# Expert tiles of the first phase in pairs: first products over 256 tokens at a time

## The chip, the cores and the metric

The kernel runs on one core of one Trainium2 chip. The metric is the device time of one launch in microseconds (us). Five engines work side by side, each through its own list of instructions in a fixed order: PE (TensorE, matrix products; the profile lists its weight loads apart as PEld), DVE (VectorE), ACT (ScalarE), POOL (GpSimd, which here also issues the gathers and scatters) and SP (SyncE, which issues most other DMAs). An instruction that has to wait holds up everything behind it on its engine.

## The reference

There are two stages. The first is a filter in the frequency domain on x of 8 batches x 2496 rows x 256 columns; the second is a mixture of 8 experts, each token going to one of them.

```python
X = rfft(x, axis=1)                              # per batch, along the 2496 rows
Yr = Xr @ w_r - Xi @ w_i + b_r ;  Yi = Xr @ w_i + Xi @ w_r + b_i
Y = shrink(Yr, 0.01) + 1j * shrink(Yi, 0.01)     # sign(v) * max(|v| - 0.01, 0)
y = irfft(Y, n=2496, axis=1)                     # 8 * 2496 = 19968 tokens of 256

e = argmax(y @ w_gate)                           # one expert of 8 for each token
for each expert e, on its own tokens y:
    h = relu(y @ w1[e])                          # 256 -> 1024: the first product
    out = gate * sigmoid(y @ w_output_gate[:, e]) * (h @ w2[e])   # 1024 -> 256: the second
```

## The kernel before

**Stages.** The transform is done as small matrix products, batch by batch, for some 580 us. Its last batch overlaps with the start of the expert stage, which then fills the rest. Filtered tokens y are stored to DRAM (`yd`); logits, the choice of expert and each token's rank in its expert are worked out per batch.

**Tiles of tokens.** The expert stage works on 163 tiles of 128 tokens (T_ALL). Each tile has tokens of one expert only; 163 is enough for any split of the 19968 tokens, and all 163 are always computed. They come in two phases. The first phase (`T_A` = 71 tiles) uses tokens of the first four batches alone, only full tiles of each expert, so that it can start while the last batches are still being transformed. The second phase (`T_B` = 92 tiles) has all other tokens. Within a phase the tiles go by expert. For each phase `routing` makes the lists of token numbers: `plan` (which expert each tile has, at which tile an expert begins), `blocks`, then for 22 columns of each batch one-hot matrices on DVE (L1129, L1130, L1149) that PE multiplies (L1157), then `indices` and `factors` on DVE. The second phase's lists are made while PE works on the first phase's tiles.

**One tile.** POOL gathers its 128 rows of y into `yg` (L1230). DVE finds a power of two per token and ACT and DVE split the row into two f16 parts, `yhl` (L1243 to L1249). SP transposes them with a DMA into `eT` (L1253). First product (`up`, L1295): two halves, each 4 chunks of 128 hidden columns by 6 matmuls. Here the weight chunk (128x128) is the stationary operand and the 128 tokens are the moving one; three f16 products stand for one precise one. Each half fills one PSUM bank of 128x512, which ACT (L1305, relu to f16) and DVE (L1306, the rest in f16) move into `hh`. Second product (L1272): 24 matmuls of 128x256, with the tokens' `hh` stationary. ACT scales the result into `o` (L1281) and POOL scatters it to `out` (L1284).

**Weights.** An expert's weights are 2 MB in f16 parts; three buffers `wbuf0` to `wbuf2` of 2 MB each hold them. Tile t uses one buffer in turn (`wplace`), so when the expert changes, each of the three must be loaded anew; the load's instruction (L1216, one for each half of 1 MB) is issued for every tile and does nothing at run time where the buffer already holds the expert (`cond=g`, the flag in `fl`). The half for the first product waits until the `up` of the tile before it in the same buffer is done, the other half until that tile's second product is done. During the first 8 tiles (`TW`) only buffers 0 and 1 are used; the third lies in memory that the transform frees.

**What sets the order.** A planner (class `Issue`) plays the work through with estimated durations while the program is built: each step asks for an engine with a due time, places in buffers are handed out by `Slots` and `Places`, and the order in which steps are served is the order in which the instructions stand on each engine. So the constants (durations, due times such as `R1`, paces such as `G1`, numbers of places) set an order at build time and nothing at run time.

With the inputs used here the first four batches have 1122, 1344, 1215, 1226, 1333, 1194, 1064 and 1486 tokens for experts 0 to 7.

Of the kernel before, what the change touches and what calls it, by code (L numbers as in the profile page):

```python
# [12 lines left out]
F16 = mybir.dt.float16  # L13
# [21 lines left out]
T_A = -((-(NA * S - E * 127)) // 128)  # L35
T_B = (N - E) // 128 + E - T_A
T_ALL = T_A + T_B

# [91 lines left out]
R1, G1 = 19.93, 1.19  # L130
# [9 lines left out]
EARLY = dict(yg=3, yhl=2, eT=2, hh=1, o=1)  # L140
PLACES = dict(yg=7, yhl=5, eT=6, hh=3, o=7)
TW = 8
# [132 lines left out]
def tile_fft_moe(ctx, tc, x, w_r, w_i, b_r, b_i, w_gate, w_og, w1, w2, f1, f4, cmat, gmat, m16, out, dbg=None):  # L275
# [147 lines left out]
    slots = {k: Slots(n) for k, n in dict(x=XR - 6, s1=S1, A=AN, xt=3, z=2, zhl=ZR, bt=1, bd=1, yt=YR, ol0=OL[0], wr=WR - 1, wsp=SR, ol1=OL[1], fac=10, dg=1).items()}  # L423
    slots.update({k: Places(range(EARLY[k])) for k in EARLY})
    give = lambda k: io.give(slots[k])
# [560 lines left out]
    def shift7(src, add, name):  # L986
        i = small(E, "s7i", I32)
        V.tensor_scalar(i, src, float(add), None, ALU.add)
        V.tensor_scalar(i, i, 7, None, ALU.arith_shift_right)
        f = small(E, name, pool=pc)  # L990
        V.tensor_copy(f, i)
        return f

    def plan(ph):

        if ph == 0:
            fl = shift7(cnt[NA - 1], 0, "fl")
            yield
            pf_ = yield from prefix(fl, "pfA")
            lim = small(E + 1, "lim", pool=pc)  # L1000
            V.tensor_scalar(lim, pf_, float(T_A), None, ALU.min)
# [4 lines left out]
        else:  # L1006
            ce = shift7(cnt[B - 1], 127, "ce")
# [16 lines left out]
        if ph == 0:  # L1024
            route["fl"] = pc.tile([1, T_ALL], I32, name="flg")
            route["ei"] = pc.tile([1, T_ALL], I32, name="ebi")
            V.memset(route["fl"][:, 0:TW + 1], 1)
        V.tensor_copy(route["ei"][:, t0:t0 + n], ev[0:1])
        if ph == 0:
            V.tensor_tensor(route["fl"][:, 2:TW], eb[0:1, 2:TW], eb[0:1, 0:TW - 2], ALU.not_equal)  # L1030
        a = max(t0, TW + 1)
        V.tensor_tensor(route["fl"][:, a:t0 + n], eb[0:1, a:t0 + n], eb[0:1, a - 3:t0 + n - 3], ALU.not_equal)
# [161 lines left out]
    def wplace(t):  # L1194
        return t % 2 if t < TW else (t - TW + 2) % 3

    def before(t):

        return None if t < 2 or t == TW else t - 2 if t < TW else t - 3

    def fetch(r):

        yield "w open"
        for t in range(T_ALL):
            yield "plan", 0 if t < T_A else 1
            if t == TW:
                yield "opened"
            for m in range(2):
                if before(t) is not None:
                    yield ("up", "down")[m], before(t)  # L1210
                def f():
# [4 lines left out]
                    nc.sync.dma_start(W[wplace(t)][:, part], wd[ds(f, 1), :, part].rearrange("a p f -> (a p) f"), cond=g, cond_hint=False)  # L1216

                new = before(t) is None
# [3 lines left out]
    def gathers(r):  # L1222
        yield "w open"
        for t in range(T_ALL):
# [6 lines left out]
            io.go(tile_(t, i, yg, r + 5.6 * t), io.now + 2.6)  # L1231

    def tile_(t, iy, yg, r):
# [3 lines left out]
        fac = small(1, "fac", bufs=10)  # L1237
# [13 lines left out]
        ie = yield slots["eT"]  # L1251
        eT = place("eT", ie, [128, 2, 2, 128], F16)
        yield from move(r - 10, 1.4e5, 1.2, lambda: nc.sync.dma_start(eT.rearrange("p v c n -> p (v c) n"), yhl.rearrange("p v d -> p (v d)"), transpose=True))  # L1253
        yield TAIL
        io.put(slots["yhl"], il)
        yield "w", t, 0
        ih = yield slots["hh"]
        hh = place("hh", ih, [128, 2, 8, 128], F16)
        w = W[wplace(t)][:, :4096].rearrange("p (c h v f) -> p c h v f", c=2, h=2, v=2)
        st["nh", t], st["nu", t] = 0, 0  # L1260
        for half in range(2):
            io.go(up(t, half, w, eT, ie, hh, r))
        yield "hh", t
        yield "w", t, 1
        w = W[wplace(t)][:, 4096:].rearrange("p (i v c d) -> p i v c d", i=4, v=2, c=2)

        def f(i):
            pt = bank(i)
            n = 0
            for fc in range(8):  # L1270
                for v, vw in ((0, 0), (0, 1), (1, 0)):
                    T.matmul(pt[:, :256], hh[:, v, fc], w[:, fc // 2, vw, fc % 2], start=(n == 0), stop=(n == 23))  # L1272
                    n += 1
            return pt

        i, pt = yield "P", r + 4, 2.61, f, True
        io.put(slots["hh"], ih)
        io.set("down", t)
        io_ = yield slots["o"]
        o = place("o", io_, [128, 256], F32)  # L1280
        yield "A", r, 0.47, lambda: A.activation(o, pt[:, :256], AF.Copy, scale=fac)  # L1281
        io.free(i)
        give("fac")
        yield "G", r, 1.0, lambda: G.indirect_dma_start(out=out, out_offset=bass.IndirectOffsetOnAxis(ap=sidx[:, t:t + 1], axis=0), in_=o, in_offset=None, bounds_check=N - 1, oob_is_err=False)  # L1284
        yield 3.6
        io.put(slots["o"], io_)

    def up(t, half, w, eT, ie, hh, r):
        def f(i):
            pt = bank(i)  # L1290
            for j in range(4):
                n = 0
                for dh in range(2):
                    for vw, v in ((0, 0), (0, 1), (1, 0)):
                        T.matmul(pt[:, 128 * j:128 * j + 128], w[:, dh, half, vw, 128 * j:128 * j + 128], eT[:, v, dh], start=(n == 0), stop=(n == 5))  # L1295
# [3 lines left out]
        i, pt = yield "P", r, 1.34, f, True  # L1299
        st["nu", t] += 1  # L1300
        if st["nu", t] == 2:
            io.put(slots["eT"], ie)
# [54 lines left out]
```

## Time and profile before

| | |
|---|---|
| time, median of 3 runs | 1557.16 us (1556.42 to 1560.42) |
| the profiled execution's own time | 1555.91 us |
| its span, first to last instruction | 1554.1 us |
| PE busy | 1440.7 us, 93% of the span |
| DVE, ACT, POOL busy | 63%, 46%, 38% |
| first matmul of the expert stage, last one | 583.2 us, 1546.7 us |
| second product of tile 63 begins | 983.8 us |

The profile was taken from one execution. Times in its rows count from the span's start. A timeline row gives start, length, engine, line of the kernel, operation, out<-in, sizes, how many instructions were merged (x24), and in brackets the idle time of that engine before it with what ended it. "issue" there means that the engine waited for nothing that the profile shows. A group row gives busy time and mean duration of one instruction, then the group's idle time by cause. Names of buffers stand without numbers (`wbuf`, `hh`, `ps` for a PSUM bank).

### The profile page before, as it was taken

Reading aid. Unit: us, or ns where it says so; the run is one execution under the profiler, and the core shown is the slowest. Engines: PE = TensorE matmul, PEld = TensorE weight load, DVE = VectorE, ACT = ScalarE, POOL = GpSimd, SP = SyncE. Lnnn points to the kernel's source line nnn. Section 1 sums busy time; section 2 is a strip of 40 time slices with the busy share of each in tenths; the row PEclk is TensorE's granted clock in tenths of the full one; section 3 lists DMA queues with packets and bytes.
Section 4 is the critical chain, followed back from the end, with each engine's and each line's share of the span. In section 5 each row is a group of like instructions: output and inputs, shape, how many; then the busy total and the mean of one; then the engine's idle time right before and its main releaser. Section 6 shows DMA issues by size and latency. Waiting matters only on the chain. (4 is left out here: it accounts for less than half of the span.)

```text
span 1554.1 us, 45643 instructions
## 1 busy us (share of the span) xinstructions
PE 1440.7 (93%) x17728; PEld 1307.6 (84%) x17728; DVE 973.0 (63%) x2910; ACT 717.0 (46%) x1385; POOL 588.0 (38%) x664
## 2 busy tenths in 40 slices
PE   4899999999899989899999999899999999999998
PEld 4789888787788768788998889788898899889897
DVE  3776777679898876566666657554454554545442
ACT  4666765758566554333333333233333333333332
POOL 0453634446263634133333232334324333333221
PEclk8899999999999999999999999999999999999999
DMA  8879999999999977958746856685673864846820
GB/s 222 200 157 222 225 224 213 208 216 218 213 202 214 201 213 166 255 122 226 228 120 181 216 152 167 202 242 158 156 215 83 230 174 132 230 122 183 216 59 19
DMA packets 330257, 287.64 MB, mean 185 GB/s; under 512 B 277734, under 2 KB 286568, under 8 KB 317753
## 3 DMA queue, kind: packets, MB, share of 16 engines
q1 hardware_dynamic: 313415, 241.50, 63.7%
q0 software_dynamic: 15648, 42.17, 10.6%
q8 instruction: 139, 2.28, 0.6%
q10 hardware_dynamic: 978, 1.06, 0.3%
q14 instruction: 77, 0.63, 0.1%
HBM read 404.52 MB, written 58.91 MB: 298 GB/s over the span
## 5 line engine op out<-in xcount | busy, mean ns | idle before, releaser
L1295 PE MATMUL ps<-eT,wbuf 128*128 128x128 f16 x7824 | 471.5, 220 | 38.3 <-issue 25.1
L1295 PEld LDWEIGHTS <-wbuf 128*128 128x128 f16 x7824 | 451.1, 98 | 52.8 <-issue 34.7
L1272 PE MATMUL ps<-wbuf,hh 128*128 128x256 f16 x3912 | 447.5, 273 | 9.9 <-issue 3.8
L1272 PEld LDWEIGHTS <-hh 128*128 128x128 f16 x3912 | 379.8, 98 | 57.7 <-issue 8.1
L1306 DVE SCALAR_TENSOR_TENSOR hh<-ps,hh 128x512 f16<-128x512 f32 x326 | 222.7, 689 | 290.2 <-ACT hh L1305 259.6
L1284 POOL DMA_INDIRECT out<-o,sidx x163 | 165.3, 1014 | 581.5 <-ACT o L1281 239.4
L1305 ACT ACTIVATE hh<-ps 128x512 f16<-128x512 f32 x326 | 191.4, 596 | 298.2 <-PE ps L1295 213.0
L668 PE MATMUL ps<-whl,xt 128*128 128x256 f16 x1920 | 229.4, 276 | 5.3 <-DVE xt L650 2.2
L668 PEld LDWEIGHTS <-xt 128*128 128x128 f16 x1920 | 190.0, 99 | 42.8 <-DVE xt L650 2.9
L1281 ACT ACTIVATE o<-ps,fac 128x256 f32<-128x256 f32 x163 | 77.1, 473 | 273.4 <-PE ps L1272 248.0
L1230 POOL DMA_INDIRECT yg<-yd,gidx x163 | 161.0, 988 | 65.0 <-issue 25.2
L1248 ACT ACTIVATE yhl<-yg,ys 128x256 f16<-128x256 f32 x163 | 81.6, 502 | 46.6 <-DVE ys L367 21.6
L1249 DVE SCALAR_TENSOR_TENSOR yhl<-yg,ys,yhl 128x256 f16<-128x256 f32 x163 | 80.8, 496 | 32.0 <-ACT yhl L1248 25.3
L586 PE MATMUL ps<-f1t,x 117*128 117x120 f32 (+1 forms) x704 | 92.5, 293 | 5.8 <-issue 4.6
L586 PEld LDWEIGHTS ps<-f1t,x 117*128 117x128 f32 (+1 forms) x704 | 89.9, 210 | 7.2 <-issue 4.7
L1243 DVE SCALAR_TENSOR_TENSOR fac<-yg,ysi,isb 128x1 f32<-128x1 f32 x163 | 36.0, 221 | 79.7 <-ACT o L1281 67.5
L687 POOL CAST zhl<-z 128x512 f16<-128x512 f32 x44 | 28.6, 652 | 138.0 <-DVE z L684 72.1
L763 PE MATMUL ps<-bdt,f4t 120*117 120x512 f16 x264 | 69.5, 385 | 7.8 <-ACT ste L714 5.8
L698 PE MATMUL ps<-gt,zhl 128*128 128x128 f16 x960 | 65.0, 219 | 10.9 <-DVE zhl L688 3.8
L698 PEld LDWEIGHTS <-zhl 128*128 128x128 f16 x960 | 57.8, 98 | 18.5 <-DVE zhl L688 4.3
L595 ACT ACTIVATE at<-ps,sx 128x480 f16<-128x480 f32 (+1 forms) x88 | 55.3, 648 | 35.6 <-PE ps L586 32.6
L683 ACT ACTIVATE zhl<-ps,sc 128x512 f32<-128x512 f32 x80 | 54.7, 686 | 37.0 <-PE ps L668 31.4
(187 smaller groups left out, 1629.4 us busy)
## 6 DMA issues: line engine op xcount, KB each, us to landing
wbuf<-wd SPq DMA_DIRECT2D x326, 1024.0 KB
yd<-yt SPq DMA_DIRECT2D x120, 158.4 KB
x<-in_x SPq DMA_DIRECT2D x120, 156.0 KB
wr<-in_moe_w SPq DMA_DIRECT2D x32, 512.0 KB
wd<-wsp SPq DMA_DIRECT2D x64, 256.0 KB
yg<-yd,gidx POOLq DMA_INDIRECT x163
eT<-yhl SPq DMA_TRANSPOSE x163
out<-o,sidx POOLq DMA_INDIRECT x163
```

The costliest lines, as they stand in the source:

```text
L586: T.matmul(pv[:, dh, :, m * j:m * j + m], xs[:k, j0 + j, 128 * dh:128 * dh + 128], fw, start=True, stop=True)
L668: T.matmul(yp[:, 256 * j:256 * j + 256], xt_[:, v, 2 * dh + j, 64 - 64 * u:192 - 64 * u], whl[:, dh, vw, 256 * u:256 * u + 256], start=Fal ...
L698: T.matmul(bv[:, j], zhl[:, vz, c:c + 128], gt[:, 2 * p + j, v], start=(n == 0), stop=(n == 2))
L1230: yield "G", r + 5.6 * t - 30, 1.0, lambda: G.indirect_dma_start(out=yg, out_offset=None, in_=src, in_offset=bass.IndirectOffsetOnAxis(ap= ...
L1248: yield "A", r - 10, 0.5, lambda: A.activation(yhl[:, 0], yg[:, :256], AF.Copy, scale=s)
L1249: yield "D", r - 10, 0.48, lambda: V.scalar_tensor_tensor(yhl[:, 1], yg[:, :256], s, yhl[:, 0], ALU.mult, ALU.subtract)
L1272: T.matmul(pt[:, :256], hh[:, v, fc], w[:, fc // 2, vw, fc % 2], start=(n == 0), stop=(n == 23))
L1281: yield "A", r, 0.47, lambda: A.activation(o, pt[:, :256], AF.Copy, scale=fac)
L1284: yield "G", r, 1.0, lambda: G.indirect_dma_start(out=out, out_offset=bass.IndirectOffsetOnAxis(ap=sidx[:, t:t + 1], axis=0), in_=o, in_of ...
L1295: T.matmul(pt[:, 128 * j:128 * j + 128], w[:, dh, half, vw, 128 * j:128 * j + 128], eT[:, v, dh], start=(n == 0), stop=(n == 5))
L1305: yield "A", r, 0.6, lambda: A.activation(hv[:, 0], pt, AF.Relu)
L1306: yield "D", r, 0.69, lambda: V.scalar_tensor_tensor(hv[:, 1], pt, 0.0, hv[:, 0], ALU.max, ALU.subtract)
```

## The change

The first phase now has 64 tiles in 32 pairs of one expert (`T_A` is counted in blocks of 256, rounded so that 32 full pairs always exist); the second phase has 99 single tiles. `BLOCKS` lists 32 blocks of two tiles and 99 of one.

- **First product of a pair** (`up` with m = 2): the moving operand is `eT` of both tiles, 256 tokens, so one matmul is 128x256 in place of two of 128x128. A pair has four quarters of 12 matmuls, each filling one PSUM bank; the ACT and DVE moves keep their size and number.
- **Second product** (`down`): unchanged, once per tile.
- **Buffers**: `eT` in 3 places of two tiles in place of 6 single ones, `hh` in 2 places of two tiles in place of 3 single ones, both cut into single places for the second phase when the last pairs leave (`back`); `o` 5 places, not 7; `yg` 6, not 7; `fac` 12, not 10. The early sets are one pair each.
- **Weights**: a block, not a tile, takes a buffer in turn (`wplace`, `before` over blocks; `KW` = 4 blocks in buffers 0 and 1). Load instructions fall from 326 to 262.
- **Lists**: `plan(0)` counts blocks of 256 (shift by 8, offsets doubled); flags compare with the block that had the buffer before. The second phase's lists are due earlier and closer together (`R1`, `G1`).

```diff
-T_A = -((-(NA * S - E * 127)) // 128)
+T_A = -((-(NA * S - E * 255)) // 256) * 2
+BLOCKS = [(t, 2) for t in range(0, T_A, 2)] + [(t, 1) for t in range(T_A, T_ALL)]
-R1, G1 = 19.93, 1.19
+R1, G1 = 0.0, 0.9
-EARLY = dict(yg=3, yhl=2, eT=2, hh=1, o=1)
-PLACES = dict(yg=7, yhl=5, eT=6, hh=3, o=7)
-TW = 8
+EARLY = dict(yg=3, yhl=2, eT=1, hh=1, o=1)
+PLACES = dict(yg=6, yhl=5, eT=3, hh=2, o=5)
+KW = 4
...
-    def wplace(t):
-        return t % 2 if t < TW else (t - TW + 2) % 3
+    def wplace(k):
+        return k % 2 if k < KW else (k - KW + 2) % 3
...
-        for t in range(T_ALL):
+        for k, (t, n) in enumerate(BLOCKS):
...
-                if before(t) is not None:
-                    yield ("up", "down")[m], before(t)
+                if before(k) is not None:
+                    yield ("up", "down")[m], BLOCKS[before(k)][0]
...
+    def block(k, r):
+        t, m = BLOCKS[k]
+        for i in range(m):
+            yield "eT", t + i
+        ie, eT = st["eT", t]
         yield "w", t, 0
...
-        for half in range(2):
-            io.go(up(t, half, w, eT, ie, hh, r))
+        for half in range(2 * m):
+            io.go(up(t, m, half, w, eT, ie, hh, r))
         yield "hh", t
         yield "w", t, 1
...
+        for i in range(m):
+            io.go(down(t + i, m, i, w, hh, ih, r + 4 * m))
...
-    def up(t, half, w, eT, ie, hh, r):
+    def up(t, m, half, w, eT, ie, hh, r):
+        c = 4 // m
         def f(i):
             pt = bank(i)
-            for j in range(4):
+            for j in range(c):
+                g = c * half + j
                 n = 0
                 for dh in range(2):
                     for vw, v in ((0, 0), (0, 1), (1, 0)):
-                        T.matmul(pt[:, 128 * j:128 * j + 128], w[:, dh, half, vw, 128 * j:128 * j + 128], eT[:, v, dh], start=(n == 0), stop=(n == 5))
+                        T.matmul(pt[:, 128 * m * j:128 * m * (j + 1)], w[:, dh, g // 4, vw, 128 * (g % 4):128 * (g % 4) + 128], eT[:, :m, v, dh], start=(n == 0), stop=(n == 5))
                         n += 1
             return pt
```

The order of the instructions moves with it. On PE the pattern of the first phase stays alike: before, both halves of two tiles, then the second products of two tiles; now the last two quarters of one pair, the first two quarters of the next, then the two second products of the first. Three other places are shown; L1216 has become L1222, L1253 L1269, L1284 L1339, L1230 L1236, L1306 L1365 in the changed kernel.

SP, where the third weight buffer gets its first load. `bdt` are the last batch's transposes for the inverse transform, ebi and flg the expert and the flag of a load. Before (buffer 2 is for tile 8; the row above it that loads buffer 1 waits for tile 5's second product):

```order
L1216 DMA wbuf1_8930<-wd_79 128x4096
L737 DMA_TRANSPOSE bdt_136<-bt_132 128x16x128
L1213 TENSOR_LOAD ebi_5821
L1213 ISA x2
L1213 TENSOR_LOAD flg_5820
L1213 ISA x2
L1216 ISA
L1216 DMA wbuf2_9194<-wd_79 128x4096
L1253 DMA_TRANSPOSE eT4_10083<-yhl0_9760 128x4x128
```

Now (buffer 2 is for block 4, tiles 8 and 9; the row that loads buffer 1 waits for the second products of block 1, tiles 2 and 3):

```order
L1222 DMA wbuf1_8931<-wd_79 128x4096
L1269 DMA_TRANSPOSE eT1_9393<-yhl4_9629 128x4x128
L1219 TENSOR_LOAD ebi_5822
L1219 ISA x2
L1219 TENSOR_LOAD flg_5821
L1219 ISA x2
L1222 ISA
L1222 DMA wbuf2_9195<-wd_79 128x4096
L739 DMA_TRANSPOSE bdt_136<-bt_132 128x8x128
L1222 ISA
L1222 DMA wbuf2_9195<-wd_79 128x4096
L739 DMA_TRANSPOSE bdt_136<-bt_132 128x16x128
```

The third buffer's load for tile 8 now stands behind the second product of tile 3, not of tile 5, and ahead of the last two `bdt` transposes, not behind them.

POOL, where the second phase's gathers begin. Before (the first row is the scatter of tile 63, the first gather that of tile 71):

```order
L1284 DMA out_0<-o0_18398,sidx_150 19968x256
L1230 DMA yg1_18424<-yd_78,gidx_149 128x260
L1230 DMA yg2_18455<-yd_78,gidx_149 128x260
L1284 DMA out_0<-o1_18451,sidx_150 19968x256
L1230 DMA yg3_18485<-yd_78,gidx_149 128x260
```

Now (the first row is the scatter of tile 53, the first gather that of tile 64):

```order
L1339 DMA out_0<-o3_15216,sidx_150 19968x256
L1236 DMA yg4_15263<-yd_78,gidx_149 128x260
L1236 DMA yg5_15299<-yd_78,gidx_149 128x260
L1236 DMA yg0_15328<-yd_78,gidx_149 128x260
L1236 DMA yg1_15331<-yd_78,gidx_149 128x260
```

The first gather stood 8 tiles behind the scatter ahead of it and stands 11 tiles behind it now.

DVE, where it first needs those gathers. Before (L1306 rows are the two halves of tile 65, L358 is tile 71's maximum):

```order
L1045 TENSOR_TENSOR isb_8931<-isb_8931,rs1_18370 128x92
L1306 SCALAR_TENSOR_TENSOR hh2_18209<-ps1_18426,hh2_18209 128x512
L358 TENSOR_REDUCE ym2_18534<-yg1_18424 128x1
L363 TENSOR_SCALAR p2c2_18540<-ym2_18534 128x1
L365 TENSOR_SCALAR p2e2_18542<-p2c2_18540 128x1
L367 TENSOR_SCALAR ys2_18544<-p2e2_18542 128x1
L369 TENSOR_SCALAR ysi2_18546<-p2e2_18542 128x1
L1243 SCALAR_TENSOR_TENSOR fac1_18535<-yg1_18424,ysi2_18546,isb_8931 128x1
L1306 SCALAR_TENSOR_TENSOR hh2_18209<-ps4_18460,hh2_18209 128x512
```

Now (L1365 rows are the last two quarters of tiles 54 and 55 and the first two of tiles 56 and 57, L359 is tile 64's maximum):

```order
L1051 TENSOR_TENSOR isb_8932<-isb_8932,rs1_15243 128x99
L1365 SCALAR_TENSOR_TENSOR hh1_9602<-ps6_15203,hh1_9602 128x512
L1365 SCALAR_TENSOR_TENSOR hh1_9602<-ps7_15226,hh1_9602 128x512
L1365 SCALAR_TENSOR_TENSOR hh0_9453<-ps0_15247,hh0_9453 128x512
L1365 SCALAR_TENSOR_TENSOR hh0_9453<-ps1_15265,hh0_9453 128x512
L359 TENSOR_REDUCE ym1_15333<-yg4_15263 128x1
```

The maximum stood between the two halves of one tile, six tiles ahead of its own; now it stands after the second quarter of the pair that is four pairs ahead of its own tile.

116 lines of the change are left out of this document (80 added, 36 removed).

## The prediction

> **What bounds the kernel now.** I read the page's busy times first, then the expert stage in stretches, then what ended PE's idle time there.
>
> ```profile
> span 1554.1 us, 45643 instructions
> PE 1440.7 (93%) x17728; PEld 1307.6 (84%) x17728; DVE 973.0 (63%) x2910; ACT 717.0 (46%) x1385; POOL 588.0 (38%) x664
> ```
>
> Stretches (length; busy time and count of PE, PEld, DVE, ACT, POOL; granted clock; DMA share, GB/s). The first is the middle of the first phase, the second the second phase:
>
> ```profile
> 668.00:984.00 316.00, 304.53 (x4019) 285.46 (x4018) 209.34 (x734) 110.77 (x215) 98.87 (x98) 0.99 0.68 184
> 1047.00:1534.00 487.00, 466.13 (x6225) 435.73 (x6222) 239.57 (x735) 174.00 (x340) 162.54 (x163) 1.00 0.59 158
> ```
>
> PE is busy 96% in both, no other engine over 66%. So PE sets the pace: a gain is matmul time that goes, or idle time of PE that goes. Its groups from 583 to 1000 us, nearly all of the first phase, name the idle time:
>
> ```profile
> L1295 PE MATMUL ps<-eT,wbuf 128*128 128x128 f16 x3216 | 199.8, 221 | 20.0 <-issue 10.9 <-DMA wbuf<-wd 8.9
> L1272 PE MATMUL ps<-wbuf,hh 128*128 128x256 f16 x1577 | 181.1, 273 | 4.1 <-DVE hh L1306 3.3 <-DMA wbuf<-wd 0.5 <-issue 0.2
> ```
>
> That is about 24 us: 9.4 for weights, 3.3 for `hh`, 11 in which the engine waited for nothing that is shown.
>
> **The change part by part.** *(a) The matmuls themselves.* A matmul's row length (219 ns) is not its price, since they overlap. The pace comes from runs without a gap:
>
> ```profile
> 583.23 2.84 PE L1295 MATMUL ps<-eT,wbuf 128*128 128x128 f16 x48
> 588.57 2.79 PE L1272 MATMUL ps<-wbuf,hh 128*128 128x256 f16 x24
> ```
>
> 48 of 128x128 take 2.84 us, so one starts every (2.84 - 0.22) / 47 = 55.7 ns; 24 of 128x256 every (2.79 - 0.27) / 23 = 109.6 ns. The weight load is hidden in both. A pair had 96 of the first kind, 5.35 us, and gets 48 of the second, 5.26 us. The saving is 0.09 us a pair; the trace's times are rounded, so 0.08 to 0.13. Over 32 pairs: **3 us** (2.5 to 4). Halving the count of matmuls saves almost nothing by itself, as each streams twice as many tokens. The second products keep number and size.
>
> *(b) Waits for weights.* The five that matter:
>
> ```profile
> 637.86 4.23 PE L1295 MATMUL ps<-eT,wbuf 128*128 128x128 f16 x48 [2.91 <-DMA wbuf<-wd]
> 654.79 2.74 PE L1295 MATMUL ps<-eT,wbuf 128*128 128x128 f16 x24 [2.82 <-DMA wbuf<-wd]
> 665.82 1.51 PE L1295 MATMUL ps<-eT,wbuf 128*128 128x128 f16 x24 [2.15 <-DMA wbuf<-wd]
> 723.49 2.78 PE L1272 MATMUL ps<-wbuf,hh 128*128 128x256 f16 x24 [0.55 <-DMA wbuf<-wd]
> 888.37 2.85 PE L1295 MATMUL ps<-eT,wbuf 128*128 128x128 f16 x48 [1.05 <-DMA wbuf<-wd]
> ```
>
> Three, 7.9 us, come when expert 1 follows expert 0 at tile 8. SP shows why the first is late:
>
> ```profile
> 626.13 2.88 SPq L737 DMA_TRANSPOSE bdt<-bt  x1
> 630.95 0.39 SPq L1216 DMA_DIRECT2D wbuf<-wd  x1
> ```
>
> The third buffer's load goes out at 630.95 behind the last inverse transpose, and PE takes it at 637.86: 6.9 us for 1 MB among other traffic. PE had been ready 2.91 us earlier. In the changed order this load stands behind the second product of tile 3 only. PE then still has two second products (2.8 us each), six quarters of 12 matmuls (1.3 us each) and the logits before it needs the load, some 16 us against 6.9. After that a block keeps its buffer for four quarters and two second products, 5.3 + 5.3 = 10.6 us, while 2 MB take about 2 x 4.7 us at 222 GB/s, the first value in the page's row of transfer rates below and one of its steady ones; a tile of 5.4 us could not cover that. What is late next are the last batch's `yd` stores, which free the two `yt` buffers for the inverse products on PE; they stand closer together there. I expect 8 of the 9.5 us to go; bounds 4 and 9.5.
>
> ```profile
> GB/s 222 200 157 222 225 224 213 208 216 218 213 202 214 201 213 166 255 122 226 228 120 181 216 152 167 202 242 158 156 215 83 230 174 132 230 122 183 216 59 19
> ```
>
> *(c) The change of phase.* PE's second product waits 3.33 us for `hh`. Followed back over DVE, POOL and ACT:
>
> ```profile
> 999.40 5.25 PE L1272 MATMUL ps<-wbuf,hh 128*128 128x256 f16 x31 [3.33 <-DVE hh L1306]
> ...
> 997.44 0.42 DVE L358 TENSOR_REDUCE ym<-yg 128x1 f32<-128x256 f32 x1 [5.50 <-DMA yg<-yd,gidx]
> 998.66 1.28 DVE L1306 SCALAR_TENSOR_TENSOR hh<-ps,hh 128x512 f16<-128x512 f32 x2
> ...
> 992.30 0.98 POOL L1284 DMA_INDIRECT out<-o,sidx  x1 [4.90 <-DMA out<-o,sidx]
> 993.59 0.99 POOL L1230 DMA_INDIRECT yg<-yd,gidx  x1 [0.30 <-issue]
> ...
> 986.60 0.47 ACT L1281 ACTIVATE o<-ps,fac 128x256 f32<-128x256 f32 x1 [2.02 <-PE ps L1272]
> ```
>
> DVE's next `hh` move stands behind the maximum of tile 71; that waits for its gather, issued at 993.59 and landed at 997.44 (3.85 us), and the gather stands behind a scatter that POOL issued 5.2 us after `o` was there (987.07). From the end of tile 63's second product to the maximum: 10.8 us. In the changed order the maximum of tile 64 stands behind two quarters of the pair 56/57. Between the end of tile 53's second product and that point PE has four quarters, 5.3 us, then ACT 0.6 and DVE 0.69: DVE is there at about 6.7 us. Without POOL's delay the gather lands at 5.6, with the same delay at 10.8. Then DVE stands still for 4 us, but its next `hh` move has no input before 5.3 + 5.3 + 1.3 = 11.9. So 3 of 3.3 us go; bounds 0 and 3.3.
>
> *(d) Pauses at issue.* They come in short series within a run:
>
> ```profile
> 595.34 0.27 PE L1295 MATMUL ps<-eT,wbuf 128*128 128x128 f16 x2 [0.40 <-issue]
> 596.07 0.33 PE L1295 MATMUL ps<-eT,wbuf 128*128 128x128 f16 x3 [0.46 <-issue]
> 596.81 0.44 PE L1295 MATMUL ps<-eT,wbuf 128*128 128x128 f16 x5 [0.41 <-issue]
> 597.64 1.34 PE L1295 MATMUL ps<-eT,wbuf 128*128 128x128 f16 x21 [0.39 <-issue]
> ```
>
> From 583 to 1000 us the first products lose 10.9 us so (64 of their 67 tiles: 10.4), the second products, with as much PE time, 0.2. The plain difference: a first product uses up two instructions (load, matmul) in 56 ns, a second in 110. I read it as instructions that arrive late while the DMAs are busy; the queue that brings them:
>
> ```profile
> q8 instruction: 139, 2.28, 0.6%
> ```
>
> 139 packets of 16.4 KB. A pair's first products run at the pace of the second. If the loss goes by instructions, half of 10.4 goes, 5.2; if by pace, 10. I take **7.5**; the lower bound is 0, for pauses that have another cause.
>
> *(e) What is added.* The second phase's lists must now be done within fewer tiles. DVE's cost of them is the difference of the two stretches: 1275 second products by their group in 668 to 984 are 53 tiles, 209.3 / 53 = 3.94 us of DVE each; from 1047 on 2092 are 87 tiles, 239.6 / 87 = 2.75.
>
> ```profile
> L1272 PE MATMUL ps<-wbuf,hh 128*128 128x256 f16 x1275 | 146.3, 273 | 0.8 <-DMA wbuf<-wd 0.5 <-issue 0.2
> L1272 PE MATMUL ps<-wbuf,hh 128*128 128x256 f16 x2092 | 236.7, 273 | 3.5 <-DMA wbuf<-wd 1.7 <-issue 1.5
> L1149 DVE TENSOR_TENSOR ob<-ob,t 117x368 f16<-117x368 f16 x40 | 13.7, 344 | 0.5
> L1157 PE MATMUL ps<-ob,ol 117*128 117x92 f16 x176 | 23.4, 261 | 1.0 <-DVE ob L1149 0.5 <-issue 0.3
> ```
>
> So 63 us of lists (5% more with 99 columns for 92), now over some 45 tiles: 2.75 + 1.47 = 4.2 us of DVE per tile of 5.5 us, 77% where it was 66%. A pair's second product starts two quarters (2.6 us) after its last quarter; the two moves take 0.6 + 0.69 us and two handovers, so 1.1 us are free for DVE's other work ahead of them, and one-hot work comes in pieces of 0.34 to 0.42. I add 1.5 us of waits; bounds 0 and 6. Fewer places for `o`: five tiles are 27 us, POOL's delay above was 5.2, no cost. 64 load instructions fewer on SP wait for nothing that PE waits for in the middle of a phase: nothing.
>
> **Sum.** 3 + 8 + 3 + 7.5 - 1.5 = 20 us. The profiled execution took 1555.9 us, 1.8 more than its span, and 1.25 less than the median of the runs. So 1535.9 for such an execution and **1537 us** for the median. All terms at their good bounds give 4 + 9.5 + 3.3 + 10 = 26.8, 1530; with pauses and waits at the bad ones (2.5 + 4 + 0 + 0 - 6) it comes to 1557.
>
> **The rivals.** *R1, the pauses stay*: they go by time under weight transfers and not by instructions. For it: the weight transfers stay, with the same experts after each other. Against it: the second products pass through the same transfers with 0.2 us. Gain 20 - 7.5 = 12.5, 1544.7 us. [...]
>
> *R2, arithmetic alone*: the weight waits move to the `yd` stores and to later experts, the change of phase finds another wait, only (a) stays. 1557.2 - 3 = 1554 us, no change that could be measured. Against it: the slack of 16 us against 6.9.
>
> *R3, slower: DVE late with `hh`.* If `hh` moves queue behind one-hot work in most of the 22 pairs under the lists, PE waits once a pair. At 1.0 us each it eats the gain of 21.5 without (e); at 1.2 us it is 26 us, and the time is 1562. For it: 77% on an engine with fixed order. Against it: now, at 66% and with the same two halves as slack, PE's whole wait for `hh` outside the change of phase is nil, and 0.5 us for one-hot matrices.
>
> *R4, more than the sum*: starts of matmuls also lose gaps too small to be listed, and all bounds are good. 1525 to 1530.
>
> **Chances.** Forecast (1530 to 1543) 0.60, R1 0.20, R2 0.07, R3 0.06, R4 0.07. Changes within 0.3% (4.7 us) can't be told from none here. Faster by more: the forecast, R1 and R4, 0.87; the same: R2, 0.07; slower: R3, 0.06. The range has to hold the forecast, R1 and a part of what lies on both sides: 1527 to 1549.
>
> **What would show it.** (a) Runs of 12 first products at 109 ns, 48 a pair in place of 96 at 56. (b) No `wbuf` wait over 1 us from 620 to 670 us, the third buffer's load out well before PE wants it; wrong if waits by `yt` or `bdt` at L765 stand there. (c) No `hh` wait over 1 us at the change of phase. (d) Issue pauses of the first products under 6 us in the first phase; if they stay at 10, R1. (e) PE's waits for `hh` and `ob` under 6 us together; over 20, R3. The second phase should keep its 5.6 us a tile (487 us for 87); if it does not, a cost lies there that I have not seen.

## The result and the profile after

The changed kernel took **1505.93 us** (median of 4, 1500.14 to 1514.79) beside 1558.79 us for the kernel before: ratio **0.9665**, 95% interval 0.9613 to 0.9717. The forecast was 1537 us, the range 1527 to 1549. So the change gained 53 us where 20 were forecast, and the time lies below the range. The profiled execution took 1500.14 us.

The page of the changed kernel, and its groups of instructions in the first phase (581 to 1000 us), in the columns of the rows shown above (L1354 is the first product, L1325 the second):

```profile
span 1498.4 us, 42257 instructions
PE 1420.1 (95%) x16192; PEld 1280.4 (85%) x16192; DVE 970.0 (65%) x2911; ACT 717.4 (48%) x1386; POOL 590.9 (39%) x664
```
```profile
L1354 PE MATMUL ps<-eT,wbuf 128*128 128x256 f16 (+1 forms) x1968 | 202.5, 261 | 1.3 <-DMA eT<-yhl 1.1 <-issue 0.2
L1325 PE MATMUL ps<-wbuf,hh 128*128 128x256 f16 x1740 | 199.3, 273 | 3.4 <-DVE hh L1365 2.0 <-issue 1.2
```

The 24 us of idle time there have become 4.7: no wait for weights, 2.0 for `hh`, 1.4 at issue. That was forecast. What was not is the second phase. The waits of PE there (what waited, for what; us in all, times, longest), of the kernel before from 1047 to 1534 us:

```profile
PE ps L1295 <- issue: 13.6, 31, 1.0
PE ps L1295 <- DMA wbuf<-wd: 3.7, 3, 2.2
PE ps L1272 <- DMA wbuf<-wd: 1.7, 2, 0.8
PE ps L1272 <- issue: 1.5, 2, 1.0
```

and of the changed one from 1006.7 to 1478:

```profile
PE ps L1354 <- DMA wbuf<-wd: 4.3, 4, 1.4
PE ps L1325 <- ACT hh L1364: 3.1, 5, 0.9
PE ps L1325 <- DVE hh L1365: 2.0, 6, 0.3
PE ps L1325 <- PE ps L1354: 0.4, 1, 0.4
```

15.1 us of pauses at issue were there before and are gone, in a phase whose products the change leaves alone. Stages by the starts of second products (us):

| kernel | tiles 0 to 10 | 10 to 60 | 60 to 73 | 73 to 160 |
|---|---|---|---|---|
| before | 79.2 | 297.4 | 81.9 | 486.6 |
| changed | 65.2 | 282.9 | 66.7 | 471.2 |

The waits view leaves out short gaps, which are booked inside a run as busy time, and counts the listed ones from a matmul's end, 0.16 us behind the point where the next one starts in a run of 128x128 (a row of 219 ns, a start every 56). A finer ledger takes the time between the starts of neighbouring matmuls and subtracts 55.8 or 109.4 ns for the expert products by their size (for others the median of their line). What is over by more than 30 ns is a "wait" where the profile names what ended it, "half clock" where the granted clock is 0.50 and the product takes up to about twice its time, and a "pause" otherwise; the rest is PE's own pace. From the first product of the expert stage to the start of tile 160's second product:

| us | pauses, up to tile 73 | pauses, after | half clock | waits | own pace | sum |
|---|---|---|---|---|---|---|
| before | 22.6 | 21.9 | 5.8 | 21.1 | 879.0 | 950.4 |
| changed | 2.5 | 0.0 | 0.0 | 17.9 | 876.5 | 896.9 |
| difference | -20.1 | -21.9 | -5.8 | -3.2 | -2.5 | -53.5 |

The granted clock was 0.50 in four stretches of 3.4 us of the kernel before, from 637.4, 654.4, 733.0 and 999.2 us on: three times where PE came back from a wait of 2.8 to 3.3 us, once behind two pauses of 1.0 us each. The changed kernel has no such stretch from 581 to 1490 us.

### The profile page after: what moved, and what is told of

It is laid out like the page before. It is cut to its first block, busy times and chain, and to the rows that moved or that the text cites. A ratio compares the mean times of both kernels' runs of the same rounds, so it can differ in the third digit from the quotient of the medians.

```text
span 1498.4 us, 42257 instructions
## 1 busy us (share of the span) xinstructions
PE 1420.1 (95%) x16192; PEld 1280.4 (85%) x16192; DVE 970.0 (65%) x2911; ACT 717.4 (48%) x1386; POOL 590.9 (39%) x664
## 2 busy tenths in 40 slices
DMA packets 329955, 285.33 MB, mean 190 GB/s; under 512 B 277702, under 2 KB 286536, under 8 KB 317721
## 5 line engine op out<-in xcount | busy, mean ns | idle before, releaser
L1354 PE MATMUL ps<-eT,wbuf 128*128 128x128 f16 (+1 forms) x6288 | 451.9, 232 | 5.6 <-DMA wbuf<-wd 4.3
L1325 PE MATMUL ps<-wbuf,hh 128*128 128x256 f16 x3912 | 444.8, 273 | 8.9 <-DVE hh L1365 4.0
L1354 PEld LDWEIGHTS <-wbuf 128*128 128x128 f16 x6288 | 419.7, 98 | 26.0 <-DMA wbuf<-wd 5.2
L1325 PEld LDWEIGHTS <-hh 128*128 128x128 f16 x3912 | 379.5, 98 | 57.0 <-DVE hh L1365 6.5
L1339 POOL DMA_INDIRECT out<-o,sidx x163 | 167.4, 1027 | 494.0 <-ACT o L1336 270.7
L1365 DVE SCALAR_TENSOR_TENSOR hh<-ps,hh 128x512 f16<-128x512 f32 x326 | 220.3, 689 | 206.7 <-ACT hh L1364 195.3
L1364 ACT ACTIVATE hh<-ps 128x512 f16<-128x512 f32 x326 | 188.3, 596 | 194.1 <-PE ps L1354 176.7
L1236 POOL DMA_INDIRECT yg<-yd,gidx x163 | 161.2, 989 | 93.2 <-DVE p2e L366 35.4
L690 POOL TENSOR_TENSOR zhl<-z,zhl 128x512 f16<-128x512 f32 x51 | 60.6, 1188 | 24.8 <-ACT zhl L688 21.4
```

Source lines behind the costliest of these rows:

```text
L1236: yield "G", r + 5.6 * t - 30, 1.0, lambda: G.indirect_dma_start(out=yg, out_offset=None, in_=src, in_offset=bass.IndirectOffsetOnAxis(ap= ...
L1325: T.matmul(pt[:, :256], hh[:, v, fc, 128 * n:128 * n + 128], w[:, fc // 2, vw, fc % 2], start=(k == 0), stop=(k == 23))
L1339: yield "G", r - 4, 1.0, lambda: G.indirect_dma_start(out=out, out_offset=bass.IndirectOffsetOnAxis(ap=sidx[:, t:t + 1], axis=0), in_=o, i ...
L1354: T.matmul(pt[:, 128 * m * j:128 * m * (j + 1)], w[:, dh, g // 4, vw, 128 * (g % 4):128 * (g % 4) + 128], eT[:, :m, v, dh], start=(n == 0) ...
L1364: yield "A", r, 0.6, lambda: A.activation(hv[:, 0], pt, AF.Relu)
L1365: yield "D", r, 0.69, lambda: V.scalar_tensor_tensor(hv[:, 1], pt, 0.0, hv[:, 0], ALU.max, ALU.subtract)
```

## The experiments

The experiments stand in five sets; each set ran on one chip of its own, with the kernel before beside it. The times turned out to differ from set to set: the kernel before took 1567.65 us (median) in set one and 1512 to 1515 in the other four. Which of the chips ran the first comparison is not recorded.

### Set one: width, order on POOL, and both

On POOL the second phase's scatters (S) and gathers (G) stood as S S G G before and stand as S G S G now. The two more places of `fac` alone decide that: with 12 in the kernel before they alternate, with 10 in the changed one they go in twos, in both phases. POOL of the changed kernel in the second phase (L1339 scatter, L1236 gather):

```profile
1197.08 1.02 POOL L1339 DMA_INDIRECT out<-o,sidx  x1 [5.02 <-ACT o L1336]
1201.30 0.98 POOL L1236 DMA_INDIRECT yg<-yd,gidx  x1 [3.21 <-DVE p2e L366]
1204.87 1.02 POOL L1339 DMA_INDIRECT out<-o,sidx  x1 [2.59 <-DMA out<-o,sidx]
```

The changed kernel once more, unchanged.

> The changed kernel once more, to see how far its time and its pauses differ from execution to execution. If the pauses at issue are set by the order on POOL, every execution has the second phase near 5.4 us a tile and no mid-run pauses in the first products: 1498 to 1510 us. If their absence in the first profile was luck, a second profile shows 10 us or more of them again and a time nearer 1520.

Measured 1511.49 us (1505.95 to 1517.55) beside 1567.65, ratio 0.9636 (0.9591 to 0.968): the gain holds, 56 us. PE's pauses in front of first products are 3.8 us in all.

The kernel before with 12 places for `fac`:

```diff
-... ol1=OL[1], fac=10, dg=1 ...
+... ol1=OL[1], fac=12, dg=1 ...
-        fac = small(1, "fac", bufs=10)
+        fac = small(1, "fac", bufs=12)
```

> The kernel before with 12 places for the tokens' factors (fac) in place of 10, nothing else: single tiles, 128-wide first products. The only visible move is on POOL, where scatters and gathers stand one by one (S G S G) where they stood in twos (S S G G). Theory POOL: the pauses at issue come when a third indirect DMA goes out within some 3 us while PE runs first products (32 of 39 such cases in the profile of before, 28.6 us, against 3 of 105 others), so this kernel loses most of the pauses: 21 of the 32 us of both phases or more, 1525 to 1537 us. Theory WIDTH: the pauses go with the instruction rate of 128-wide products, so they stay: 1553 to 1560. Theory ORDER OF THE REST: the gain of the second phase has a cause in the buffers of hh; no change either.

Measured 1564.69 us, ratio 0.9991 (0.9952 to 1.003): no gain in all. But in the profile, which caught the fastest of its ten runs (1550.32 us), the second phase (tiles 73 to 160) took 470.1 us, 16.5 less than in the profile of before; the first phase took 82.9 (0 to 10), 304.4 (10 to 60) and 87.6 (60 to 73), 16.4 more. PE's waits over the whole run have new ones at the one-hot products, and the pauses stay, all but 0.8 us of them ahead of 1057 us:

```profile
PE ps L1295 <- issue: 18.8, 29, 1.9
PE ps L1295 <- DMA wbuf<-wd: 10.1, 4, 4.3
PE ps L1157 <- DVE ob L1149: 9.0, 9, 3.3
```

The changed kernel with 10 places (the same edit backwards):

> The changed kernel with 10 places for the factors, as before the change; on POOL scatters and gathers stand in twos again in both phases. Theory POOL: the pauses come back in the second phase, where the first products are 128 wide, 13 to 20 us; in the first phase, with 256-wide products at half the instruction rate, few come back: 1518 to 1530 us. Theory WIDTH: no change, 1500 to 1510.

Measured 1540.29 us, ratio 0.9819 (0.9765 to 0.9873): 28.8 us slower than the changed kernel on this chip, all of it behind tile 60 (74.9 and 498.4 us, where the changed kernel had 67.4 and 477.8 in this set). By the ledger pauses rise by 27.4 us; in the second phase waits for weights rise by 4.8 and those for `hh` fall by 7.7.

The changed kernel whose pairs multiply 128 tokens at a time:

```diff
-                for dh in range(2):
-                    for vw, v in ((0, 0), (0, 1), (1, 0)):
-                        T.matmul(pt[:, 128 * m * j:128 * m * (j + 1)], ..., eT[:, :m, v, dh], ...)
+                for i_ in range(m):
+                    n = 0
+                    for dh in range(2):
+                        for vw, v in ((0, 0), (0, 1), (1, 0)):
+                            T.matmul(pt[:, 128 * (m * j + i_):128 * (m * j + i_) + 128], ..., eT[:, i_, v, dh], ...)
```

> The changed kernel with pairs, buffers and order as they are, but a pair's first products done as two matmuls of 128 tokens each, as many matmuls and weight loads as before the change. Theory POOL: only the matmuls' own time comes back, 0.09 to 0.13 us a pair, 3 to 4 us, since POOL's order stays one by one: 1503 to 1512 us. Theory WIDTH: the pauses of the first phase come back too, 8 to 11 us on top: 1511 to 1522.

Measured 1529.82 us, ratio 0.9779 (0.9727 to 0.9831): 18.3 us slower than the changed kernel. Tiles 10 to 60 took 295.1 us against 283.4, with 8.1 us of issue pauses at the first products of the first phase; waits for weights in that phase were none. So in the first phase the pairs took the weight waits away, the width the pauses.

The kernel before took some 9 us more in this set than in the first comparison, and all four kernels came out above the times expected of them. What is read here is differences within the set.

**What the pauses follow.** Most stand where POOL issues indirect DMAs close together. The profile of before in the second phase, POOL and then PE:

```profile
1174.30 1.01 POOL L1284 DMA_INDIRECT out<-o,sidx  x1 [2.96 <-ACT yhl L1248]
1175.62 0.99 POOL L1230 DMA_INDIRECT yg<-yd,gidx  x1 [0.30 <-DVE p2e L365]
1176.91 0.96 POOL L1230 DMA_INDIRECT yg<-yd,gidx  x1 [0.30 <-DMA out<-o,sidx]
1178.18 1.02 POOL L1284 DMA_INDIRECT out<-o,sidx  x1 [0.30 <-issue]
```
```profile
1175.78 2.42 PE L1295 MATMUL ps<-eT,wbuf 128*128 128x128 f16 x40
1178.55 0.44 PE L1295 MATMUL ps<-eT,wbuf 128*128 128x128 f16 x5 [0.36 <-issue]
1179.99 1.22 PE L1295 MATMUL ps<-eT,wbuf 128*128 128x128 f16 x19 [1.00 <-issue]
```

I call a DMA a third one when two others started within 3.2 us before it, and ask how many third ones that start while PE is in first products have a pause within 1.25 us. Profile of before: 11 of 13 in tiles 10 to 60 (9.2 us), 21 of 26 in the second phase (19.4 us); while PE is in second products, 2 of 28. The changed kernel with 10 places, in this set: none of 15 in tiles 10 to 60, whose products are 256 wide, and 21 of 27 in the second phase (20.8 us). With another rule for border cases the first two counts are 14 of 16 and 20 of 24.

By that rule alternating is not enough by itself: in tiles 10 to 73 of the kernel before with 12 places POOL alternates too, yet 19 third DMAs fall into first products, where the profile of before has 17, and 14 of them have a pause. In its second phase there is one, where there were 24. So where there are pauses, they go with the width and with how close POOL's DMAs stand; the pairs avoid them, and the alternating order does where it spaces the DMAs out. That the third DMA itself is the cause is argued from these counts.

### Set two: another chip

Here the kernel before took **1513.59 us** (13 runs, 1510.77 to 1521.81), 54 us less than in set one.

The kernel before with fills between POOL's DMAs in the second phase:

```diff
+            def apart(t):
+                if t >= T_A:
+                    G.memset(bt[:, 0:8], 0.0)
-            yield "G", ..., lambda: G.indirect_dma_start(...)
+            yield "G", ..., lambda: apart(t) or G.indirect_dma_start(...)
```

> The kernel before, with a fill of eight columns on POOL (about 1 us) ahead of each scatter and each gather of the second phase. The order on POOL stays two scatters, two gathers; only their distance grows from about 1 us to about 2. Theory 'density' (a 128-wide first product pauses when a third indirect DMA starts on POOL within some 3 us): no three starts lie within 3.2 us any more, pauses in the middle of runs in the second phase fall from 19.9 us to under 6, the stretch from the second product of tile 73 to that of tile 160 falls from 487 to about 471 us, the first phase keeps its time (82 and 297 us), about 1542 against 1557: ratio 0.990. Rival 'order' (what helps in the changed kernel is that scatter and gather alternate, so that o, yg or the weight buffers come free at other times): the stretch stays at 485 to 490, ratio 1.00. Slower than before by more than 3 us would say that the later scatters hold up o.

Measured 1548.83 us, ratio 1.0263 (1.0221 to 1.0305): slower. Neither theory was tested: in the first phase, which this edit leaves alone, 14 third DMAs fell into first products and none had a pause. On this chip there was nothing to remove, and the fills cost time, by a path shown in set four.

The kernel before, first products over 64 of the 128 rows (half of the sum over d is left out, so its result is another):

```diff
-T.matmul(..., w[:, dh, half, vw, 128 * j:128 * j + 128], eT[:, v, dh], ...)
+T.matmul(..., w[0:64, dh, half, vw, 128 * j:128 * j + 128], eT[0:64, v, dh], ...)
```

> The kernel before, whose first products take only the first 64 of the 128 rows of weights and tokens (half of the sum over d is left out, so the result is another; all instructions keep their number and order). Each load of weights and each matmul reads half as much. Theory 'operands' (POOL's bursts and the 128-wide products compete for reading the buffers that hold weights and tokens): the pauses in the second phase fall from 19.9 us to under 12. Theory 'instructions' (the pause goes with the number of instructions in a time, whatever they read): they stay between 16 and 24 us, with some 80% of the third starts in first products followed by a pause. In both the matmuls start every 56 ns as before.

Measured 1538.43 us, with no third DMA followed by a pause (0 of 43 in the two stretches), for the same reason: the theories are not told apart.

The changed kernel with 64 more weight loads whose condition is always false:

```diff
+            V.memset(route["fl"][:, T_ALL:T_ALL + 1], 0)
...
+                    if n == 2:
+                        nc.sync.dma_start(wx, wd[ds(f, 1), :, part]..., cond=st["z"], cond_hint=False)
```

(`wx` is an unused 1 MB in DRAM, st["z"] the value of the new column.)

> The changed kernel with one more conditional weight load of 1.05 MB behind each of the 64 of the first phase, whose condition is always false: as many conditional loads as in the kernel before. Theory 'a skipped load still reads': HBM read rises by 67 MB from 337.4 to 404.5 MB, bytes moved by the queues stay at 285 MB. Rival: it stays at 337. On time: if the 64 skipped loads were part of what the change gained, the stretch from the second product of tile 10 to that of tile 60 rises from 283 us towards the 297 of before and the ratio from 0.965 to 0.975; I expect no change (within 3 us, ratio 0.963 to 0.969), as PE waits for weights in neither.

Measured 1506.6 us (10 runs, 1498.46 to 1511.34). Tiles 10 to 60 took 281.3 us, as in the changed kernel's four profiles (281.8 to 283.9), so the skipped loads cost nothing that shows there. The start of the stage (tiles 0 to 10) took 72.4 us against 65.2 to 69.3 in the changed kernel's four profiles, with one wait of 4.3 us for `yt`; one profile can't tell whether the loads or the spread made that. The memory counter is taken up at the end.

The changed kernel with the due times of the lists as before:

```diff
-R1, G1 = 0.0, 0.9
+R1, G1 = 19.93, 1.19
```

> The changed kernel with the two due-time constants of the second phase's lists put back (19.93 and 1.19). The change of phase (second product of tile 60 to that of tile 73) took 82 us before and 67 now. If the due times made that gain: 75 to 85 us and the ratio up by 0.005 to 0.01. If the pairs made it (the loop over pairs has its products before the change ready in another order): 65 to 70 us and the same ratio as the changed kernel on this chip. I expect the second.

Measured 1493.74 us, ratio 0.9878 (0.983 to 0.9927); the change of phase took 67.6 us. The due times did not make its gain.

### Set three: the profile of before where it takes 1513 us

> The kernel before, unchanged, profiled on this chip. On the chip of the first runs it took 1556 to 1576 us and paused after triples of indirect DMAs in both phases; on another chip the same kernel took 1511 to 1522, and kernels with its first phase showed no such pause there (14 triples in first products, 0 pauses). So the pause is thought to belong to the chip and the kernel together. Expected: either about 1560 with 25 to 45 us of pauses in the middle of runs behind first up, or about 1513 with under 12 us of them; a time of 1513 with the pauses, or of 1560 without, would say that something else differs between the chips.

Measured 1512.12 us, on a third chip. Second phase 467.5 us; third DMAs in first products: 0 of 14 and 0 of 29 with a pause. A like place to the one above, POOL and PE; the 96 first products of two tiles run through:

```profile
1154.60 1.01 POOL L1284 DMA_INDIRECT out<-o,sidx  x1 [4.47 <-ACT yhl L1248]
1155.92 0.99 POOL L1230 DMA_INDIRECT yg<-yd,gidx  x1 [0.30 <-DVE p2e L365]
1157.21 0.97 POOL L1230 DMA_INDIRECT yg<-yd,gidx  x1 [0.30 <-DMA out<-o,sidx]
1158.48 1.02 POOL L1284 DMA_INDIRECT out<-o,sidx  x1 [0.30 <-ACT hh L1305]
```
```profile
1156.09 5.52 PE L1295 MATMUL ps<-eT,wbuf 128*128 128x128 f16 x96
```

The program and its order are the same, and so are the four distances on POOL; what differs is the chip and the moment of the run. In place of pauses PE waits for weights. Its waits from 571 to 1022 us:

```profile
PE ps L1295 <- DMA wbuf<-wd: 14.5, 8, 3.7
PE ps L1272 <- DMA wbuf<-wd: 3.0, 2, 2.2
PE ps L1272 <- DVE hh L1306: 3.0, 1, 3.0
```

17.5 us for weights, where the first profile had 9.4 in that phase. I read it so that a PE not held up by pauses reaches the loads sooner; no run isolates that.

> The kernel before with first products over 64 of 128 rows (half of the sum over d left out), on the same chip as the profile of the unchanged one. If that one pauses here: theory 'operands' says that this one does not (second phase under 8 us of pauses), theory 'instructions' says that it pauses as much (16 to 24 us). If the unchanged one does not pause here, neither does this, and nothing is told apart.

Measured 1525.92 us; again nothing is told apart.

> The changed kernel on this chip. If the kernel before pauses here: ratio 0.960 to 0.970. If it does not (1513 us): only what the prediction's parts (a) to (c) give stays, 14 us less some waits, so 1497 to 1503 us, ratio 0.989 to 0.994.

Measured **1498.04 us** beside 1513.48: ratio **0.9871** (0.9801 to 0.9942). The changed kernel's waits from 581 to 1007 us on this chip have no weights in them:

```profile
PE ps L1325 <- DVE hh L1365: 2.2, 4, 1.0
PE ps L1354 <- DMA eT<-yhl: 2.0, 1, 2.0
```

> The changed kernel with the due times of the second phase's lists as before (19.93, 1.19), beside the changed kernel on one chip. On the other chip it took 1489 to 1504 us, where the changed kernel with 64 skipped loads more took 1498 to 1511. If the due times are worth something by themselves, it is faster than the changed kernel by 5 to 12 us here too, by fewer waits for weights and hh in the second phase (2.1 us there against 7 to 10); if not, within 4 us of it.

Measured 1496.67 us, ratio 0.9886 (0.982 to 0.9952): equal to the changed kernel on the same chip. The 1493.74 of set two was no gain of the due times.

### Set four: a fourth chip

> The kernel before, profiled on the chip of this call. With pauses: some 1560 us, 80% of the third indirect DMAs in first products followed by one, 17 to 24 us of pauses in the second phase. Without: some 1513 us, none.

Measured 1513.85 us; second phase 463.6 us; 0 of 14 and 0 of 28 third DMAs with a pause.

> The kernel before with first products over 64 of 128 rows (half of the sum over d left out). If the chip shows pauses in the unchanged kernel: 'operands' says under 8 us of them in the second phase, 'instructions' 16 to 24 us. If it shows none, none here either.

Measured 1543.53 us, and here too nothing is told apart.

> The kernel before with a fill of 1 us on POOL ahead of each scatter and gather of the second phase. If the chip shows pauses: they stay in the first phase (8 to 14 us) and go in the second (under 5 us), where some 20 us of waits for hh come instead, as on the other chip. If not: some 1540 us again, by those waits alone.

Measured 1544.72 us, as on the other chip, and the second phase 493.8 against 463.6 us. With the fills POOL has no slack (L1224 is the fill), DVE stands at the maximum of a tile whose gather is late, and the `hh` moves behind it make PE wait. POOL, then DVE's wait and PE's from 1030 us on:

```profile
1106.16 1.02 POOL L1288 DMA_INDIRECT out<-o,sidx  x1 [0.17 <-ACT o L1285]
1107.16 0.99 POOL L1224 MEMSET bt<- 128x1024 f16 x1
1109.44 1.01 POOL L1288 DMA_INDIRECT out<-o,sidx  x1 [1.29 <-ACT o L1285]
1110.43 0.98 POOL L1224 MEMSET bt<- 128x1024 f16 x1
1111.57 1.00 POOL L1234 DMA_INDIRECT yg<-yd,gidx  x1 [0.16 <-DVE yhl L1253]
```
```profile
DVE ym L358 <- DMA yg<-yd,gidx: 96.7, 24, 10.5
PE ps L1276 <- DVE hh L1310: 23.8, 8, 5.5
```

> The kernel before with two more places for fac, so that scatter and gather alternate on POOL. If the chip shows pauses: second phase near 470 us against 487 of the unchanged kernel. If not: the order has nothing left to remove, and the second phase takes 465 to 475 us as in the unchanged kernel there (467).

Measured 1532.95 us where the kernel before took 1513: second phase 467.8, no better than 463.6. The alternating order alone removes nothing here. In this one profile the kernel is 19 us slower: it begins the expert stage 8.3 us later, which may be spread, and takes 5.8 us more for tiles 10 to 60 and 4.2 for the second phase.

### Set five: a fifth chip, the order on POOL once more

> The changed kernel beside the one with ten places for fac. On a chip without pauses: 1498 us or so, ratio 0.985 to 0.994, second phase 468 to 473 us with 9 to 12 us of pauses and waits. On a chip with them: ratio 0.960 to 0.970.

Measured **1499.55 us** (10 runs) beside 1514.65 (19 runs): ratio **0.9913** (0.9875 to 0.9951).

> The changed kernel with ten places for fac instead of twelve, so that scatters and gathers go in twos again. On a chip without pauses the twos cost nothing: second phase 464 to 470 us, the kernel equal to the changed one or up to 6 us faster. If the alternation is worth something by itself, it is 5 us or more slower there. On a chip with pauses: 25 to 30 us slower, as on the first chip.

Measured 1499.14 us, ratio 0.9892 (0.9857 to 0.9927): equal. In set one the same two kernels were 28.8 us apart. PE's waits of this kernel in the second phase, set one and then set five:

```profile
PE ps L1354 <- issue: 18.1, 39, 1.3
PE ps L1354 <- DMA wbuf<-wd: 6.1, 4, 3.4
PE ps L1325 <- DMA wbuf<-wd: 3.4, 3, 1.7
PE ps L1325 <- issue: 0.9, 3, 0.4
```
```profile
PE ps L1354 <- DMA wbuf<-wd: 4.5, 3, 2.0
PE ps L1325 <- DMA wbuf<-wd: 3.5, 3, 2.4
PE ps L1325 <- ACT o L1336: 0.6, 1, 0.6
```

0 of 30 third DMAs had a pause, where 21 of 27 had.

## Why the prediction was right and wrong

**The two sums.** The gain has two parts. One was there in sets three and five, where the kernel before does not pause: 15.4 us and 15.1 by the medians; the interval of the latter is 7.4 to 18.9 us. The other is pauses, and is there only where the kernel before has them: 42.0 us of the 53.5 in the ledger. The forecast without (d) was 12.5 us, inside that interval, but in part by luck: more was gained at the weights and more lost at `hh` than forecast. With (d) it was 20, and the profile from which it was made came from a chip with pauses.

- **(a) matmul time, 3 us: right.** Products of 128x256 start every 109 ns. PE's own pace fell by 2.5 us in the ledger of the first comparison and by 2.0 in that of set three.
- **(b) weights, 8 of 9.5: right that they go, too small where there are no pauses.** No wait for weights is left in the first phase in the changed kernel's rows above, and none either when the pairs multiply 128 wide: so it is the pairs, by their slower turn of buffers or the earlier load, and not the width. In set three 17.5 us went. A cost was missed here: the prediction's own rows show 48 first products in 4.23 us and 24 in 2.74 behind two of these waits, where 48 take 2.84 and 24 take 1.51, and 31 second ones in 5.25 behind the wait of (c), where 24 take 2.79. Those are the stretches at half clock, 5.8 us in the ledger; one of the four followed pauses, and all are gone in the changed kernel's profile.
- **(c) change of phase, 3 of 3.3: right.** The wait of 3.33 us is gone; waits of PE for DVE's `hh` are 2.0 us in the whole first phase, the longest 1.0. The stretch from tile 60 to 73 fell by 15.2 us, but 5.4 of that only says that two tiles' first products fewer stand between these marks; some 4 are pauses, the rest the wait and the half clock behind it. In set three, without pauses, it fell by 10.2.
- **(d) pauses, 7.5 us in the first phase: the step that failed.** On the chip of the first comparison the ledger has 20.1 us gained in that phase and 21.9 in the second. Three things in it were wrong. *Place*: the loss was priced from the rows of 583 to 1000 us alone; from 1047 on I read 96% busy and the row of the second products and concluded that "the second phase should keep its 5.6 us a tile". The row of the first products there, 13.6 us at issue, was in the same view. That phase took 471 us, 5.4 a tile. *Size*: 10.9 us of listed idle time stood for 16.3 between the first products' starts, and 3.3 more lay between second products behind 1000 us. *Cause*: I read it as late instructions. In the second phase before, 8 of 19 series of pauses have an instruction packet within 3 us ahead, and such windows cover 32% of the time, so 6 would by chance. The pauses go with POOL's third DMA. That the width makes the products immune was right (none of 15 in set one, and they come back at width 128).
- **The edit I passed over.** `fac` 12 for 10 stands in the change's list of buffers, and the prediction has no term for it. It is what alternates POOL's order, and with pauses 28.8 us hung on it; without, nothing. In the kernel before alone its profile gained 16.5 us in the second phase and lost as much in the first.
- **(e) added waits, 1.5: too small.** PE's waits for `hh` over the whole changed run are 7.1 us (4.0 for DVE, 3.1 for ACT), above the bound of 6, and 9.4 in set three. 5.1 of the 7.1 stand in the second phase, where the term saw no cost; the kernel before had none there.
- **The rivals.** R1 was wrong that the pauses stay. R3 did not come. R4 was nearest, but its small gaps account for only a part.

**What stays open.** What differs between the chips is not shown, nor that it is the chip: each was visited in one sitting only, so something else at that time is not ruled out. The three profiles of the kernel before begin the stage at 583.2 (with pauses), 571.5 and 577.7 us, with a granted clock of 0.98 and 287.64 MB moved in each. Nor is it known what in PE stops: the kernel with half the rows would have told operands from instructions, but ran three times on chips without pauses. Whether DMAs merely further apart avoid them was not tried where they occur. No variant was shown to beat the changed kernel.

## What to carry to other kernels

Idle time at issue that follows another engine's bursts may be absent in the next run on another chip: price it as a term of its own, and say what the gain is without it (here 53 us with, 15 without). Read the groups of every phase, also of the one that a change leaves alone, and take the pace from starts of instructions rather than from busy shares. A number of places that seems to add only slack can reorder a queue; look at that queue's order before giving it no cost.

## What the runs showed of the hardware

- **Pauses in some runs.** With 128x128 products every 56 ns, a third indirect DMA on POOL within 3.2 us was followed by a pause of PE of some 0.9 us in 32 of 39 cases in the profile of the first comparison, and in 0 of 85 in the two profiles of the same program in sets three and four. The kernel before took 1556 to 1576 us in the first comparison and set one, and 1503 to 1525 in sets two to five.
- **Half clock behind a stop.** Where PE came back from waits of 2.8 to 3.3 us in the first profile, the granted clock was 0.50 for 3.4 us: 48 first products took 4.23 us behind one of these waits and 2.84 elsewhere.
- **The memory counter rises with skipped loads.** Changed kernel, then with 64 skipped loads of 1.05 MB more:

```profile
HBM read 337.41 MB, written 58.91 MB: 264 GB/s over the span
HBM read 404.52 MB, written 126.02 MB: 353 GB/s over the span
```

Both columns rise by 67.1 MB, the queues' 285.33 MB not at all. So here this row holds bytes that no queue moved; the kernel before reads 404.52 too, with 64 loads more than the changed one. Whether the memory itself was accessed is not shown.

- **First products over 64 rows.** With 64-row first products among 128-row second ones, the first start after a change from one to the other comes at 148 ns in place of 56, and at 205 in place of 109: 92 to 96 ns a change. That kernel took 1538.43, 1525.92 and 1543.53 us where the kernel before took 1512 to 1514 (medians). What PE does in those 92 to 96 ns is not shown.
